# Where x is loaded and its statistics are made, in a fused forward and backward pass of an adaLN block with a 2-D Fourier filter

## The chip, the cores and the metric

The kernel runs on one core of a Trainium2 chip. The metric is the device time of one execution in microseconds (us); a run of the kernel is compared by its median. An engine is named as the profile names it: PE is TensorE's matmuls, PEld its weight loads, DVE is VectorE, ACT is ScalarE, POOL is GpSimd, SP is SyncE, which here only issues DMAs. Each engine takes its instructions from a queue of its own, in order.

## The reference

One block of a network, on 2048 tokens of 1024 channels, and its gradients for one grad_out. The inputs are bfloat16.

```
sa, ca, ga, sb, cb, gb = six rows of silu(c) @ w_mod
h = layernorm(x) * (1 + ca) + sa
x = x + ga * irfft2(rfft2(h) * (w_r + 1j * w_i))
h = layernorm(x) * (1 + cb) + sb
y = x + gb * (gelu(h @ w1 + b1) @ w2 + b2)
out = y and the gradients of y with respect to x, w_r, w_i, w1, b1, w2, b2, c, w_mod
```

w1 is 1024 by 3584. The two-dimensional Fourier transforms are made as matmuls with matrices of sines and cosines.

## The kernel before, in words

Tokens are worked in four tiles of 512 (128 partitions, 4 groups, 1024 channels). The program is written as one long list; a scheduler puts it into one fixed queue per engine, by the order in which the program has it, by priorities, and by what depends on what. `tc.issue_after(ins)` puts the instructions under it behind `ins`; `tc.high_priority()` draws them ahead.

**Loads at the start (SP's queue).** `mod_get`/`mod_load` (L269–271) bring half blocks of w_mod, 1 MB each, into the tiles wblk, of which there are three in a ring; `mod_block` (L273–284) multiplies such a half block by silu(c) on PE (the tile in PSUM is pm) and casts it into a row (L282). `load_tok` (L140–148) brings one of the four tiles of x, `x4s[0..3]` (x_0 to x_3 in the rows): half of it, 512 KB, by a plain DMA of SP (L144), and the rest in two gathers that POOL issues (L146). `load_go` (L351) brings one of four tiles of grad_out, 1 MB each: go0 and go1 have tiles of their own, the last two lie in `fbuf[:, 2]` and `fbuf[:, 3]`. `load_w2t` (L342) brings chunks of w2, transposed, into wt. Blocks 1 (1 + ca, `opca_row`) and 5 (gb, `gb_row`) of w_mod are needed first.

**The turns of grad_out.** gb's row is turned into a column (pc, L381; gb_col, L383). Then each tile of grad_out is transposed by 32 matmuls on PE (pt, L389), and every fourth finishes a bank of PSUM, which DVE (L393) and ACT (L397) by turns scale with gb_col and write to gBoT. The last turn's results let PE begin with pp: `ph_part` (L834–847) multiplies gBoT with w2's chunk `fc`, and ACT or DVE evicts the result (L845, into pho or phr). Seven chunks (fc 0 to 6) are ordered ahead of the spectral part; the rest, from L922 on, have no fixed place, and the scheduler lays them between later work. The other blocks of w_mod (pm) lie between them.

**The sines.** `trig` (L434–448, called ten times by `gen_mats`, L454–471) makes a matrix in three steps: POOL writes rows of indices (L419) into one of two buffers gidx, DVE takes them modulo a power of two by an AND (L446), ACT takes the sine (L447). Two small sines more make al (L467). A sine and a square root need different tables on ACT, which an ACT_TABLE_LOAD brings.

**Statistics and folds.** The loop at L862 goes over the four tiles of x. `ln_dve` makes mean and variance with BN_STATS on DVE (L493), `ln_mix` makes half of them so (L503) and half with two passes of ACT (L507, L510), `ln_act` all with ACT; each ends in `ln_fin`, with one Sqrt on ACT (L483) and two small operations on DVE. `norm_act` (L518) normalises on ACT into fbuf. The first tile takes `ln_dve`, the others `ln_mix`. Then DVE multiplies by `opca_row` and folds (all TENSOR_TENSORs of L195): `fold_tok` and `fold_d` or `fold_pair`, with x's tile as scratch, and at the end of each pair the row saf is added. A fold here is the sums and differences of mirrored tokens and channels that quarter the Fourier matmuls.

**The spectral part.** `spectral_core` begins with `s_fwd` (L531): pu (L542 for the matrices CE and SE, kept in smA) multiplies folded tiles by sines; CE's first pu are ordered behind the last pp of chunk 6 (`early_pe`, L541). After it come pcs (L581), the filter, pv and po (L774), and `consume_fwd` (L885), which adds to x, normalises twice on DVE and ACT, and writes n3 for the MLP. While it runs, PE has pp to do.

Of the kernel before, what the change touches and what calls it, by code (L numbers as in the profile page):

```python
# [35 lines left out]
def kernel(  # L36
# [39 lines left out]
    def ps_d(name):  # L76
        return psum.tile([P, 512], FP32, tag="d", name=name)
# [116 lines left out]
    def tt(out, a, b, op):  # L194
        return nc.vector.tensor_tensor(out=out, in0=a, in1=b, op=op)  # L195
# [154 lines left out]
    def load_go(j):  # L350
        nc.sync.dma_start(out=gos[j], in_=go_f[j * BW:(j + 1) * BW, :].rearrange("(a p) d -> p a d", p=P))  # L351
# [3 lines left out]
    def mod_get(r, h):  # L355
        wm[r, h] = mod_tile()
        mod_load(r, h, wm[r, h][:], nc.sync)

    mod_get(1, 0)
    load_tok(x4s[0], A_x, 0)  # L360
    mod_get(1, 1)
    mod_get(5, 0)
    for h in range(2):
        mod_block(1, h, wm[1, h][:])
# [13 lines left out]
    load_w2t(3)  # L378
    pc = ps_d("pc")
    for cch in range(NDC):  # L380
        nc.tensor.matmul(pc[:, cch:cch + 1], lhsT=gb_row[0:1, cch * P:(cch + 1) * P], rhs=ones_bf[0:1, 0:1], start=True, stop=True)  # L381
# [56 lines left out]
    def trig(dst, colv, rowv, nrow, width, modn, cosine):  # L438
        idx = gidx[:, gcount[0] % 2, :]
        gcount[0] += 1  # L440
        sh = float(3 * modn // 4 if cosine else modn // 2)
        for r in range(nrow):
            ov = idx[:, r * width:(r + 1) * width]
            pts(ov.rearrange("p (s w) -> p s w", s=2) if len(colv.shape) == 3 else ov, colv, rowv[r], sh, ALU.mult, ALU.add)
        n = nrow * width
        nc.vector.tensor_scalar(out=idx[:, 0:n], in0=idx[:, 0:n], scalar1=modn - 1, scalar2=None, op0=ALU.bitwise_and)  # L446
        nc.scalar.activation(out=dst, in_=idx[:, 0:n].rearrange("p (r w) -> p r w", w=width), func=ACT.Sin,  # L447
                             bias=negpi[:], scale=2 * np.pi / modn)
# [5 lines left out]
    def gen_mats():  # L454
        for cl, colv, modn in ((CE, kev, 2048), (SE, kev, 2048), (CO, kod, 4096), (SO, kod, 4096)):
            sm = (smA, smB)[cl % 2]
            rows, n = (rowo, 4) if cl % 2 else (rowe, 2)
            if cl == SE:
                nc.gpsimd.memset(kev[:, 0:1], 512.0)
            for r in range(0, n, 2):  # L460
                trig(sm[:, cl // 2, r:r + 2, :], colv, rows[r:r + 2], 2, 512, modn, cl < 2)
            if n == 2:
                nc.gpsimd.dma_start(out=d_SF[:, cl, 0:n], in_=sm[:, cl // 2])
        for cl, colv, modn in ((CE, jf[:, 0:256], 1024), (SE, jf[:, 1:257], 1024), (CO, jod, 2048), (SO, jod, 2048)):
            trig(em1[:, 0, 2 * cl:2 * cl + 2, :], colv, rowe, 2, 256, modn, cl < 2)
# [7 lines left out]
    def ln_act(x4, row, i, jk):  # L473
        sv = small.tile([P, 4, 4], FP32, tag="lnsv")
        for q in range(4):
            nc.scalar.activation(out=jk[:, q, :], in_=x4[:, q, :], func=ACT.Identity, accum_out=sv[:, q, 0:1])
        nc.vector.tensor_scalar(out=sv[:, :, 1:2], in0=sv[:, :, 0:1], scalar1=-1.0 / D, scalar2=None, op0=ALU.mult)
        for q in range(4):
            nc.scalar.activation(out=jk[:, q, :], in_=x4[:, q, :], func=ACT.Square, bias=sv[:, q, 1:2], accum_out=sv[:, q, 2:3])
        ln_fin(sv[:, :, 2:3], sv[:, :, 1:2], sv[:, :, 3:4], 1.0 / D, row, i)  # L480

    def ln_fin(var, nmean, std, scale, row, i):
        sqrt_in[0] = nc.scalar.activation(out=std, in_=var, func=ACT.Sqrt, bias=eps_c[:], scale=scale)  # L483
        rs = stats[:, row, 0, 4 * i:4 * i + 4].rearrange("p (q o) -> p q o", o=1)
        nc.vector.reciprocal(out=rs, in_=std)
        tt(stats[:, row, 1, 4 * i:4 * i + 4].rearrange("p (q o) -> p q o", o=1), nmean, rs, ALU.mult)

    def ln_dve(x4, row, i):
        st = small.tile([P, 4, 2, nc.vector.BN_STATS_DIM], FP32, tag="lnst", bufs=1)
        mv = small.tile([P, 4, 4], FP32, tag="lnmv")  # L490
        for q in range(4):
            for h in range(2):
                nc.vector.bn_stats(out=st[:, q, h, :], in_=x4[:, q, h * KH:(h + 1) * KH])  # L493
            nc.vector.bn_aggr(out=mv[:, q, 0:2], in_=st[:, q])
        nc.vector.tensor_scalar(out=mv[:, :, 2:3], in0=mv[:, :, 0:1], scalar1=-1.0, scalar2=None, op0=ALU.mult)
        ln_fin(mv[:, :, 1:2], mv[:, :, 2:3], mv[:, :, 3:4], 1.0, row, i)

    def ln_mix(x4, row, i, jk):
        st = small.tile([P, 4, 2, nc.vector.BN_STATS_DIM], FP32, tag="lnst", bufs=1)
        mv = small.tile([P, 4, 4], FP32, tag="lnmv")  # L500
        for q in range(2):
            for h in range(2):
                nc.vector.bn_stats(out=st[:, q, h, :], in_=x4[:, q, h * KH:(h + 1) * KH])  # L503
            nc.vector.bn_aggr(out=mv[:, q, 0:2], in_=st[:, q])
        nc.vector.tensor_scalar(out=mv[:, 0:2, 2:3], in0=mv[:, 0:2, 0:1], scalar1=-1.0, scalar2=None, op0=ALU.mult)
        for q in range(2, 4):
            nc.scalar.activation(out=jk[:, q, :], in_=x4[:, q, :], func=ACT.Identity, accum_out=mv[:, q, 0:1])  # L507
        nc.vector.tensor_scalar(out=mv[:, 2:4, 2:3], in0=mv[:, 2:4, 0:1], scalar1=-1.0 / D, scalar2=None, op0=ALU.mult)
        for q in range(2, 4):
            nc.scalar.activation(out=jk[:, q, :], in_=x4[:, q, :], func=ACT.Square, bias=mv[:, q, 2:3], accum_out=mv[:, q, 0:1])  # L510
        nc.vector.tensor_scalar(out=mv[:, 2:4, 1:2], in0=mv[:, 2:4, 0:1], scalar1=1.0 / D, scalar2=None, op0=ALU.mult)
        ln_fin(mv[:, :, 1:2], mv[:, :, 2:3], mv[:, :, 3:4], 1.0, row, i)

    def norm_act(out4, in4, row, i):
        norm_in[0] = ()
        for q in range(4):
            t = 4 * i + q
            norm_in[0] += (nc.scalar.activation(out=out4[:, q, :], in_=in4[:, q, :], func=ACT.Identity,  # L518
                                                scale=stats[:, row, 0, t:t + 1], bias=stats[:, row, 1, t:t + 1]),)

    sqrt_in, norm_in = [None], [()]
# [1175 lines left out]
```

## Time and profile before

| | us |
|---|---|
| time, median of 3 runs | 1399.26 (1396.29 to 1399.28) |
| the profiled execution: its time | 1398.61 |
| the profiled execution: its span | 1396.8 |
| PE busy in the span | 1351.6 |
| DVE busy | 1063.7 |
| ACT busy | 767.6 |
| POOL busy | 347.8 |
| TensorE clock granted, mean | 0.99 |

The span is what the profile sees, from its first instruction to its last; the rest of the execution's time lies around it. Busy times of different engines overlap. "PE pu L542 <- DVE fbuf L195" in a list of waits reads: PE's matmul of line 542, which writes pu, waited for DVE's instruction of line 195, which writes fbuf. In a timeline a row gives start, length, engine, line, operation, output<-input, shapes, how many in a run, and in brackets the idle time ahead and what ended it.

### The profile page before, as it was taken

Reading aid. Unit: us, or ns where it says so; the run is one execution under the profiler, and the core shown is the slowest. Engines: PE = TensorE matmul, PEld = TensorE weight load, DVE = VectorE, ACT = ScalarE, POOL = GpSimd, SP = SyncE. Lnnn points to the kernel's source line nnn. Section 1 sums busy time; section 2 is a strip of 40 time slices with the busy share of each in tenths; the row PEclk is TensorE's granted clock in tenths of the full one; section 3 lists DMA queues with packets and bytes.
Section 4 is the critical chain, followed back from the end, with each engine's and each line's share of the span. In section 5 each row is a group of like instructions: output and inputs, shape, how many; then the busy total and the mean of one; then the engine's idle time right before and its main releaser. Section 6 shows DMA issues by size and latency. Waiting matters only on the chain.

```text
span 1396.8 us, 18464 instructions
## 1 busy us (share of the span) xinstructions
PE 1351.6 (97%) x6774; PEld 657.6 (47%) x6899; DVE 1063.7 (76%) x1471; ACT 767.6 (55%) x1090; POOL 347.8 (25%) x434
## 2 busy tenths in 40 slices
PE   4998999999999999999999999999999999999998
PEld 2545566444444444444444444444654555444444
DVE  4997889977888787787811388889888489976990
ACT  4875657657977766656503684445732454534311
POOL 5410533301212122122111011011444320332351
PEclk8999999999999999999999999999999999999999
DMA  9982755899787777697999979988679978899991
GB/s 318 289 237 57 202 143 189 259 273 357 241 246 247 229 248 239 202 275 247 244 319 219 220 185 272 306 275 231 216 221 259 222 205 200 218 232 239 292 344 64
DMA packets 360689, 331.12 MB, mean 237 GB/s; under 512 B 207962, under 2 KB 303088, under 8 KB 360470
## 3 DMA queue, kind: packets, MB, share of 16 engines
q1 hardware_dynamic: 319702, 204.96, 56.9%
q0 software_dynamic: 35136, 119.73, 25.0%
q10 hardware_dynamic: 5760, 5.25, 1.2%
q8 instruction: 54, 0.88, 0.3%
q14 instruction: 37, 0.30, 0.1%
HBM read 165.73 MB, written 114.87 MB: 201 GB/s over the span
## 4 chain that ended last, share of the span: by engine, by line
PE 72%; DVE 7%; DMA 3%; issue 1%; ACT 1%; ACTq 0%; DVEq 0%
PE pg L1130 14%; PE gw1acc L1565 13%; PE gw2acc L1302 13%; PE pz L976 13%; PE pbo L1030 13%; DVE ct L195 4%; PE pp L839 2%; PE po L774 1%; DVE st L493 1%; PE pcs L581 1%; DMA hhsA<-d_hh 1%; DMA w2sA<-in_B_w_dram 1%; DMA d_n<-ct 1%; PE acc3a L218 1%; PE pu L542 1%
## 5 line engine op out<-in xcount | busy, mean ns | idle before, releaser
L839 PE MATMUL pp<-gBoT,wt 128*128 128x512 bf16 x874 | 197.9, 383 | 4.1 <-ACT phr L845 2.9
L1130 PE MATMUL pg<-w1T,gzr 128*128 128x512 bf16 x877 | 194.3, 379 | 1.3 <-issue 0.5
L1565 PE MATMUL gw1acc<-gzh,n3n 128*128 128x512 bf16 x626 | 139.1, 379 | 3.6 <-DVE ct L779 2.8
L839 PEld LDWEIGHTS <-wt 128*128 128x128 bf16 x896 | 88.0, 98 | 108.2 <-issue 7.3
L1565 PEld LDWEIGHTS <-n3n 128*128 128x128 bf16 x896 | 87.4, 98 | 108.2 <-issue 4.4
L1130 PEld LDWEIGHTS <-gzr 128*128 128x128 bf16 x896 | 86.6, 98 | 108.4 <-issue 5.8
L976 PEld LDWEIGHTS <-w 128*128 128x128 bf16 x896 | 87.3, 98 | 106.8 <-issue 2.4
L976 PE MATMUL pz<-n3Tb,w 128*128 128x512 bf16 x437 | 98.4, 379 | 1.6 <-DVE w2sD L1052 0.9
L976 PE MATMUL pz<-n3Ta,w 128*128 128x512 bf16 x439 | 98.0, 379 | 0.4
L195 DVE TENSOR_TENSOR ct<-ct 128x2048 bf16<-128x2048 bf16 (+1 forms) x84 | 91.6, 1119 | 7.1 <-DMA d_n<-ct 4.7
L1030 PEld LDWEIGHTS <-hhA 128*128 128x128 bf16 x608 | 58.9, 98 | 72.7 <-issue 2.5
L1302 PE MATMUL gw2acc<-gB,hhsA 128*128 128x512 bf16 x405 | 91.7, 379 | 0.6
L1569 ACT CAST gwo<-gw1acc 128x512 bf16<-128x512 f32 x56 | 32.2, 581 | 108.3 <-PE gw1acc L1565 87.8
L979 ACT ACTIVATE gt<-pz,b_col 128x512 bf16<-128x512 f32 x112 | 72.9, 682 | 33.3 <-PE pz L976 33.0
L987 ACT ACTIVATE gt<-gt 128x2048 bf16<-128x2048 bf16 x28 | 53.5, 1911 | 64.3 <-DVE gt L195 64.3
L195 DVE TENSOR_TENSOR gt<-gt,gt 128x2048 bf16<-128x2048 bf16 x56 | 68.6, 1224 | 19.8 <-ACT gt L989 18.5
L1310 ACT CAST gwo<-gw2acc 128x512 bf16<-128x512 f32 x40 | 23.6, 590 | 85.8 <-PE gw2acc L1302 85.8
L1302 PEld LDWEIGHTS <-hhsA 128*128 128x128 bf16 x416 | 40.7, 98 | 47.2
L1565 PE MATMUL gw1acc<-gzu,n3n 128*128 128x512 bf16 x251 | 55.2, 379 | 0.3
L983 ACT ACTIVATE gt<-gt 128x2048 bf16<-128x2048 bf16 x28 | 53.5, 1909 | 2.3 <-DVE hhC L195 1.6
L989 ACT ACTIVATE gt<-gt 128x2048 bf16<-128x2048 bf16 x28 | 53.4, 1907 | 0.4
L1302 PE MATMUL gw2acc<-gB,otl 128*128 128x512 bf16 x218 | 49.2, 379 | 0.4 <-issue 0.2
(371 smaller groups left out, 2511.0 us busy)
## 6 DMA issues: line engine op xcount, KB each, us to landing
gzr<-d_gz SPq DMA_DIRECT2D x28, 512.0 KB
wblk<-in_w_mod_dram SPq DMA_DIRECT2D x12, 1024.0 KB
d_ph<-pho POOLq DMA_DIRECT2D x21, 512.0 KB, 5.6
out_dram<-otl POOLq DMA_DIRECT2D x40, 256.0 KB, 4.8
d_hh<-hhA POOLq DMA_DIRECT2D x19, 512.0 KB, 5.0
wrw<-in_w_mod_dram SPq DMA_DIRECT2D x32, 256.0 KB
w<-in_B_w_dram SPq DMA_DIRECT2D x7, 1024.0 KB
hhC<-d_ph SPq DMA_DIRECT2D x14, 512.0 KB
```

The lines of the kernel that those rows point to most:

```text
L195: return nc.vector.tensor_tensor(out=out, in0=a, in1=b, op=op)
L839: last_pe[0] = nc.tensor.matmul(pp[:], lhsT=wt[:, fc % 4, cch, :], rhs=gBoT[j][:, cch, :], start=(cch == 0), stop=(cch == NDC - 1))
L976: last_pe[0] = nc.tensor.matmul(pz[:], lhsT=w1s[g][:, cch, k * P:(k + 1) * P], rhs=n3T[:, cch, :], start=(cch == 0), stop=(cch == NDC - 1))
L979: z_in = nc.scalar.activation(out=zb[:, k, :], in_=pz[:], func=ACT.Identity, bias=b1_col[:, fc:fc + 1], scale=1.0)
L983: nc.scalar.activation(out=av, in_=zb, func=ACT.Square)
L987: nc.scalar.activation(out=sg, in_=bv, func=ACT.Sigmoid, scale=2.0 * GK)
L989: nc.scalar.activation(out=bv, in_=bv, func=ACT.Sigmoid, scale=-2.0 * GK)
L1030: last_pe[0] = nc.tensor.matmul(pbs[i][:], lhsT=hh[:, k, i * P:(i + 1) * P], rhs=wp[:, k, :], start=False, stop=(g == 6 and k == 3))
L1130: last_pg[0] = nc.tensor.matmul(pgs[i][:], lhsT=gzs[b, g][:, k, i * P:(i + 1) * P], rhs=w1Ts[g][:, k, h * KH:(h + 1) * KH], start=(g == 0 ...
L1302: nc.tensor.matmul(acc[:], lhsT=hh_of(fc)[:, t, :], rhs=gBs[t // 4][:, t % 4, h * KH:(h + 1) * KH], start=(t == 0), stop=(t == NT - 1))
L1565: nc.tensor.matmul(acc[:], lhsT=n3ns[t // 4][:, t % 4, cch * P:(cch + 1) * P], rhs=gz2[t // 8][:, t % 8, :], start=(t == 0), stop=(t == NT ...
L1569: w1g["ev"] = nc.scalar.copy(out=ob, in_=acc[:])
```

## The change

The plain halves of all four tiles of x go ahead of gb's half blocks and grad_out in SP's queue. The functions for the statistics move up in the program, and all four tiles' statistics stand ahead of the turns: the second tile's on ACT alone (`ln_act`), the others' on DVE alone (`ln_dve`); `ln_mix` is left for later parts. The first two tiles are normalised there too, the last two in the loop of the folds. Every sine of `trig` and of al is ordered behind `x_sqrt`, the last square root of these statistics.

```
@@ loads
+    load_tok(x4s[0], A_x, 0)
     mod_get(1, 0)
-    load_tok(x4s[0], A_x, 0)
+    load_tok(x4s[1], A_x, 1)
     mod_get(1, 1)
+    load_tok(x4s[2], A_x, 2)
+    load_tok(x4s[3], A_x, 3)
     mod_get(5, 0)
     for h in range(2):
         mod_block(1, h, wm[1, h][:])
...
     load_go(0)
     load_w2t(0)
     load_w2t(1)
-    load_go(1)
-    load_tok(x4s[1], A_x, 1)
-    load_go(2)
-    load_go(3)
+    for j in range(1, 4):
+        load_go(j)
     for h in range(2):
         mod_block(5, h, wm[5, h][:])
-    load_tok(x4s[2], A_x, 2)
-    load_tok(x4s[3], A_x, 3)
     load_w2t(2)
     load_w2t(3)
...
+    for i in range(4):
+        if i == 1:
+            ln_act(x4s[i], 0, i, fbuf[:, i])
+        else:
+            with tc.issue_after(u_in.ins):
+                ln_dve(x4s[i], 0, i)
+    x_sqrt = sqrt_in[0]
+    for i in range(2):
+        norm_act(fbuf[:, i], x4s[i], 0, i)
     pc = ps_d("pc")
@@ trig
-        nc.scalar.activation(out=dst, in_=idx[:, 0:n].rearrange("p (r w) -> p r w", w=width), func=ACT.Sin,
-                             bias=negpi[:], scale=2 * np.pi / modn)
+        with tc.issue_after(x_sqrt.ins):
+            nc.scalar.activation(out=dst, in_=idx[:, 0:n].rearrange("p (r w) -> p r w", w=width), func=ACT.Sin,
+                                 bias=negpi[:], scale=2 * np.pi / modn)
@@ gen_mats
         for k in range(2):
-            nc.scalar.activation(out=al[:, k, :], in_=rown, func=ACT.Sin, scale=np.pi / (2048 << k))
+            with tc.issue_after(x_sqrt.ins):
+                nc.scalar.activation(out=al[:, k, :], in_=rown, func=ACT.Sin, scale=np.pi / (2048 << k))
@@ loop of the folds
-        if i == 0:
-            with tc.issue_after(u_in.ins):
-                ln_dve(x4, 0, i)
-        elif i > 0:
-            ln_mix(x4, 0, i, fb)
-        else:
-            ln_act(x4, 0, i, fb)
-        norm_act(fb, x4, 0, i)
+        if i > 1:
+            norm_act(fb, x4, 0, i)
         tt(fb, fb, bcn(opca_row, 4), ALU.mult)
         fold_tok(fb, x4)
```

What this does to the queues is seen at three places. First SP, from its first load of w_mod on, before; x_0 to x_3 are the tiles of x, go_142 and go_143 the first two of grad_out, fbuf its last two:

```order
L271 DMA wblk<-in_w_mod_dram 128x8x512
L144 DMA x_0_137<-in_A_x_dram 128x2x1024
L271 DMA wblk<-in_w_mod_dram 128x8x512 x2
L351 DMA go_142<-in_grad_out_dram 128x4x1024
L271 DMA wblk<-in_w_mod_dram 128x8x512
L342 DMA_TRANSPOSE wt<-in_B_w_dram 128x8x128 x2
L351 DMA go_143<-in_grad_out_dram 128x4x1024
L144 DMA x_1_138<-in_A_x_dram 128x2x1024
L351 DMA fbuf<-in_grad_out_dram 128x4x1024 x2
L144 DMA x_2_139<-in_A_x_dram 128x2x1024
L144 DMA x_3_140<-in_A_x_dram 128x2x1024
L342 DMA_TRANSPOSE wt<-in_B_w_dram 128x8x128 x2
```

And the same place of the changed kernel:

```order
L144 DMA x_0_137<-in_A_x_dram 128x2x1024
L271 DMA wblk<-in_w_mod_dram 128x8x512
L144 DMA x_1_138<-in_A_x_dram 128x2x1024
L271 DMA wblk<-in_w_mod_dram 128x8x512
L144 DMA x_2_139<-in_A_x_dram 128x2x1024
L144 DMA x_3_140<-in_A_x_dram 128x2x1024
L271 DMA wblk<-in_w_mod_dram 128x8x512 x2
L351 DMA go_142<-in_grad_out_dram 128x4x1024
L342 DMA_TRANSPOSE wt<-in_B_w_dram 128x8x128 x2
L351 DMA go_143<-in_grad_out_dram 128x4x1024
L351 DMA fbuf<-in_grad_out_dram 128x4x1024 x2
L342 DMA_TRANSPOSE wt<-in_B_w_dram 128x8x128 x2
```

Four plain halves of x stand ahead of all of grad_out now, where one did; go_142 went behind the last half block of gb.

Second DVE, among the folds of the first pair of tiles, before. The TENSOR_TENSORs are folds, the CASTs are evictions of pp, the rest are statistics of the third tile, x_2:

```order
L195 TENSOR_TENSOR fbuf<-x_0_137 128x2048
L508 TENSOR_SCALAR mv<-mv 128x2
L503 BN_STATS st<-x_2_139 128x6
L845 CAST pho<-pp 128x4x128
L195 TENSOR_TENSOR x_0_137<-fbuf 128x4x512 x2
L511 TENSOR_SCALAR mv<-mv 128x2
L504 BN_AGGR mv<-st 128x2
L195 TENSOR_TENSOR fbuf<-x_0_137 128x8x256
L845 CAST pho<-pp 128x4x128
L195 TENSOR_TENSOR fbuf<-x_0_137 128x8x256
L485 RECIPROCAL stats<-mv 128x4
L503 BN_STATS st<-x_2_139 128x6
```

In the changed kernel, where every line of the functions below `pc` is about ten higher (the AND is L504, the eviction of pp L855):

```order
L195 TENSOR_TENSOR fbuf<-x_0_137 128x2048
L195 TENSOR_TENSOR fbuf<-fbuf,rows_86 128x4096
L504 TENSOR_SCALAR gidx<-gidx 128x1024
L855 CAST pho<-pp 128x4x128
L504 TENSOR_SCALAR gidx<-gidx 128x1024
L195 TENSOR_TENSOR x_0_137<-fbuf 128x4x512
L855 CAST pho<-pp 128x4x128
L504 TENSOR_SCALAR gidx<-gidx 128x512 x2
L855 CAST pho<-pp 128x4x128
L195 TENSOR_TENSOR x_0_137<-fbuf 128x4x512
L504 TENSOR_SCALAR gidx<-gidx 128x512 x2
L195 TENSOR_TENSOR fbuf<-x_0_137 128x8x256 x2
```

The statistics are gone from between the folds, and ANDs of the sines stand there. Between the last turn of grad_out and the last fold stand 2 BN_STATS where 9 stood, 8 ANDs (4 of 1024 and 4 of 512 elements) where 6 stood (2 and 4), and 6 evictions of pp where 10 stood.

Third PE, at the begin of the spectral part, before; pp of the last chunk ahead of it, then the first pu:

```order
L839 LDWEIGHTS wt
L839 MATMUL pp<-gBoT_135,wt 128x512
L542 LDWEIGHTS fbuf
L542 MATMUL pu<-smA,fbuf 128x256
L542 LDWEIGHTS fbuf
L542 MATMUL pu<-smA,fbuf 128x256
L839 LDWEIGHTS wt
L839 MATMUL pp<-gBoT_132,wt 128x512
```

Behind these two pu stand 39 pp, and then the other six pu of this tile of PSUM. In the changed kernel (pp is L849, pu L552):

```order
L849 LDWEIGHTS wt
L849 MATMUL pp<-gBoT_135,wt 128x512
L552 LDWEIGHTS fbuf
L552 MATMUL pu<-smA,fbuf 128x256
L552 LDWEIGHTS fbuf
L552 MATMUL pu<-smA,fbuf 128x256
L552 LDWEIGHTS fbuf
L552 MATMUL pu<-smA,fbuf 128x256
L552 LDWEIGHTS fbuf
L552 MATMUL pu<-smA,fbuf 128x256
```

All eight pu stand together, and the next pp behind them. The number of pp is the same in all; 51 more of them stand in the long block beside `consume_fwd` (512 where 461 stood).

More of the change, by code (lines that the diff above doesn't have):

```diff
@@ L368, with ln_act @@
     load_w2t(1)
-    load_go(1)
-    load_tok(x4s[1], A_x, 1)
-    load_go(2)
-    load_go(3)
+    for j in range(1, 4):
+        load_go(j)
     for h in range(2):
         mod_block(5, h, wm[5, h][:])
-    load_tok(x4s[2], A_x, 2)
-    load_tok(x4s[3], A_x, 3)
     load_w2t(2)
     load_w2t(3)
+    def ln_act(x4, row, i, jk):
+        sv = small.tile([P, 4, 4], FP32, tag="lnsv")
+        for q in range(4):
+            nc.scalar.activation(out=jk[:, q, :], in_=x4[:, q, :], func=ACT.Identity, accum_out=sv[:, q, 0:1])
+        nc.vector.tensor_scalar(out=sv[:, :, 1:2], in0=sv[:, :, 0:1], scalar1=-1.0 / D, scalar2=None, op0=ALU.mult)
+        for q in range(4):
+            nc.scalar.activation(out=jk[:, q, :], in_=x4[:, q, :], func=ACT.Square, bias=sv[:, q, 1:2], accum_out=sv[:, q, 2:3])
+        ln_fin(sv[:, :, 2:3], sv[:, :, 1:2], sv[:, :, 3:4], 1.0 / D, row, i)
@@ new lines, in ln_fin, with ln_dve @@
+    def ln_fin(var, nmean, std, scale, row, i):
+        sqrt_in[0] = nc.scalar.activation(out=std, in_=var, func=ACT.Sqrt, bias=eps_c[:], scale=scale)
+        rs = stats[:, row, 0, 4 * i:4 * i + 4].rearrange("p (q o) -> p q o", o=1)
+        nc.vector.reciprocal(out=rs, in_=std)
+        tt(stats[:, row, 1, 4 * i:4 * i + 4].rearrange("p (q o) -> p q o", o=1), nmean, rs, ALU.mult)
+    def ln_dve(x4, row, i):
+        st = small.tile([P, 4, 2, nc.vector.BN_STATS_DIM], FP32, tag="lnst", bufs=1)
+        mv = small.tile([P, 4, 4], FP32, tag="lnmv")
+        for q in range(4):
+            for h in range(2):
+                nc.vector.bn_stats(out=st[:, q, h, :], in_=x4[:, q, h * KH:(h + 1) * KH])
+            nc.vector.bn_aggr(out=mv[:, q, 0:2], in_=st[:, q])
+        nc.vector.tensor_scalar(out=mv[:, :, 2:3], in0=mv[:, :, 0:1], scalar1=-1.0, scalar2=None, op0=ALU.mult)
+        ln_fin(mv[:, :, 1:2], mv[:, :, 2:3], mv[:, :, 3:4], 1.0, row, i)
@@ new lines, in ln_mix @@
+    def ln_mix(x4, row, i, jk):
+        st = small.tile([P, 4, 2, nc.vector.BN_STATS_DIM], FP32, tag="lnst", bufs=1)
+        mv = small.tile([P, 4, 4], FP32, tag="lnmv")
+        for q in range(2):
+            for h in range(2):
+                nc.vector.bn_stats(out=st[:, q, h, :], in_=x4[:, q, h * KH:(h + 1) * KH])
+            nc.vector.bn_aggr(out=mv[:, q, 0:2], in_=st[:, q])
+        nc.vector.tensor_scalar(out=mv[:, 0:2, 2:3], in0=mv[:, 0:2, 0:1], scalar1=-1.0, scalar2=None, op0=ALU.mult)
+        for q in range(2, 4):
+            nc.scalar.activation(out=jk[:, q, :], in_=x4[:, q, :], func=ACT.Identity, accum_out=mv[:, q, 0:1])
+        nc.vector.tensor_scalar(out=mv[:, 2:4, 2:3], in0=mv[:, 2:4, 0:1], scalar1=-1.0 / D, scalar2=None, op0=ALU.mult)
+        for q in range(2, 4):
+            nc.scalar.activation(out=jk[:, q, :], in_=x4[:, q, :], func=ACT.Square, bias=mv[:, q, 2:3], accum_out=mv[:, q, 0:1])
+        nc.vector.tensor_scalar(out=mv[:, 2:4, 1:2], in0=mv[:, 2:4, 0:1], scalar1=1.0 / D, scalar2=None, op0=ALU.mult)
+        ln_fin(mv[:, :, 1:2], mv[:, :, 2:3], mv[:, :, 3:4], 1.0, row, i)
@@ new lines, in norm_act @@
+    def norm_act(out4, in4, row, i):
+        norm_in[0] = ()
+        for q in range(4):
+            t = 4 * i + q
+            norm_in[0] += (nc.scalar.activation(out=out4[:, q, :], in_=in4[:, q, :], func=ACT.Identity,
+                                                scale=stats[:, row, 0, t:t + 1], bias=stats[:, row, 1, t:t + 1]),)
+    sqrt_in, norm_in = [None], [()]
+    for i in range(4):
[4 more added lines that the diff above has]
+                ln_dve(x4s[i], 0, i)
@@ L471, in gen_mats @@
         nc.gpsimd.dma_start(out=d_E[:], in_=em1[:])
[L473 to L521, printed above, removed]
     def behind(ins, later):
```

## The prediction

> **What bounds the kernel now.** I read the page's engine line and its slices first, then PE's waits, because PE is nearly always busy.
>
> ```profile
> PE 1351.6 (97%) x6774; PEld 657.6 (47%) x6899; DVE 1063.7 (76%) x1471; ACT 767.6 (55%) x1090; POOL 347.8 (25%) x434
> ...
> PE   4998999999999999999999999999999999999998
> ...
> PEclk8999999999999999999999999999999999999999
> ```
>
> PE is busy for 1351.6 of 1396.8 us, and its matmuls are the same in both kernels. So the change can move the time only through PE's 45 idle us and through the stretches in which PE is granted a lower clock. The waits from 0 to 330 us hold most of that idle time:
>
> ```profile
> PE pm L279 <- DMA wblk<-in_w_mod_dram: 12.0, 5, 4.6
> PE pu L542 <- DVE fbuf L195: 4.0, 1, 4.0
> PE pp L839 <- ACT phr L845: 2.9, 1, 2.9
> ...
> PE pt L389 <- DMA go<-in_grad_out_dram: 2.0, 1, 2.0
> ...
> PE pt L389 <- DMA fbuf<-in_grad_out_dram: 0.7, 1, 0.7
> ```
>
> The columns are total, times and longest. Three places can move: the loads ahead of the transposes (pt), the wait of the spectral part (pu) for the folds, and the late wait of pp for an eviction by ACT. The timeline of PE shows them in order of time:
>
> ```profile
> 33.17 3.75 PE L389 MATMUL pt<-ident,go 128*128 128x128 bf16 x32 [2.03 <-DMA go<-in_grad_out_dram]
> 37.66 6.18 PE L389 MATMUL pt<-ident,fbuf 128*128 128x128 bf16 x64 [0.74 <-DMA fbuf<-in_grad_out_dram]
> 43.83 5.34 PE L839 MATMUL pp<-gBoT,wt 128*128 128x512 bf16 x23
> 49.63 1.89 PE L279 MATMUL pm<-wblk,u_b 128*128 128x512 bf16 x8 [0.46 <-DMA wblk<-in_w_mod_dram]
> ...
> 101.09 7.07 PE L839 MATMUL pp<-gBoT,wt 128*128 128x512 bf16 x32
> ...
> 108.21 8.58 PE L839 MATMUL pp<-gBoT,wt 128*128 128x512 bf16 x38
> 120.77 1.46 PE L542 MATMUL pu<-smA,fbuf 128*128 128x256 bf16 x6 [3.97 <-DVE fbuf L195]
> ```
>
> Up to 43.83 PE follows grad_out's tiles as they land. From there it has pp enough until 116.8, and waits 3.97 us for the last fold. Three windows (length; then PE, PEld, DVE, ACT and POOL busy; clock; DMA share; GB/s) say who is full and where:
>
> ```profile
> 20.00:40.00 20.00, 13.57 (x108) 9.72 (x107) 13.98 (x38) 13.86 (x26) 5.36 (x8) 0.67 1.04 334
> 44.37:120.71 76.34, 70.69 (x323) 31.80 (x327) 72.76 (x108) 51.10 (x76) 20.78 (x26) 0.99 0.78 223
> 120.77:134.00 13.23, 13.20 (x87) 9.67 (x88) 5.94 (x7) 8.62 (x15) 0.00 (x0) 0.78 0.00 0
> ```
>
> From 20 to 40 us the DMA engines are full at 334 GB/s. From the last turn of grad_out (44.37) to the last fold (120.71) DVE is busy for 72.76 of 76.34 us, so DVE sets when the spectral part starts. Behind the wait PE runs 13.23 us at .78 of its clock.
>
> **Term 1, the loads.** Ahead of grad_out's last tile now stand the plain halves of x2 and x3, 0.52 MB each, which stood behind it. The halves that POOL gathers are issued from POOL's own queue in both kernels. So 1.05 MB more goes through full DMA engines at 334 GB/s: +3.1 us. SP's transposes of w2 move too, and go1 is queued behind them as before; gb's second half block has only 0.5 MB more ahead of it, which is the lower bound, 1.6 us. The upper one is 4.7, if x1's half, ahead of go2 already, counts again. I take 3.1, since the DMA share is 1.04: the last fbuf transposes come 3.1 us late, pp starts at 46.9 instead of 43.8, and DVE comes to its folds at 47.5 instead of 44.4. The statistics that now lie ahead of the turns go into DVE's and ACT's idle time (6 us each of the 20 in the window, and more before it), so I count them at nothing; without that cover eleven BN_STATS by 0.67 us, 7 us, would stand ahead of the turns.
>
> **Term 2, DVE from the turns to the last fold.** Groups of DVE from 44.37 to 120.77 (busy, mean ns | idle before):
>
> ```profile
> L503 DVE BATCH_NORM_STATS2 st<-x 128x6 f32<-128x512 bf16 x9 | 6.0, 679 | 0.0
> L845 DVE CAST pho<-pp 128x512 bf16<-128x512 f32 x8 | 5.5, 683 | 0.0
> ...
> L446 DVE TENSOR_SCALAR gidx<-gidx 128x512 int32<-128x512 int32 x4 | 1.7, 427 | 2.3 <-POOL gidx L419 2.3
> ...
> L446 DVE TENSOR_SCALAR gidx<-gidx 128x1024 int32<-128x1024 int32 x2 | 1.4, 691 | 0.0
> L504 DVE BATCH_NORM_AGGREGATE mv<-st 128x2 f32<-128x12 f32 x5 | 1.0, 201 | 0.0
> L508 DVE TENSOR_SCALAR mv<-mv 128x2 f32<-128x2 f32 x3 | 0.5, 150 | 0.0
> ```
>
> Nine BN_STATS become two: −7 × 0.67 = −4.7. Aggregates go from five to two (−0.6), and of three sets of small operations like L508's, five of 0.16 to a set, one of three is left (−2.0). DVE's evictions of pp ahead of the last fold go from ten to six: −4 × 0.68 = −2.7. One cast of a mod block goes to ACT (−0.7). Two more of the wide ANDs for the sines come behind the turns: +2 × 0.69 = +1.4; small work on al that waited for a sine comes behind too, some +0.8 by the 0.15 to 0.2 us of such operations. Sum −8.5: 64.3 us of work, which from 47.5 ends at 111.8 if nothing waits.
>
> **The added wait.** Ten sines, all ordered behind the last Sqrt of x, leave two index buffers full until then; eight ANDs then stand among the folds in DVE's queue, and behind each the rest of the folds. In the trace before, four do, and they wait 2.3 us in all:
>
> ```profile
> DVE gidx L446 <- POOL gidx L419: 2.3, 4, 0.9
> DVE fbuf L195 <- ACT fbuf L518: 1.1, 1, 1.1
> ```
>
> By that mean, 0.57 us, eight wait 4.6; the bounds are 0 (the rows are ready in time) and 10.8 (the narrow ones wait the longest, 0.9, and the wide ones, with twice the elements, 1.8). I take 4.6, the mean of what stands nearest. The 1.1 us for ACT's normalised tile I keep, since two of the tiles are still normalised beside the folds. The last fold ends at 111.8 + 4.6 + 1.1 = **117.5**, 3.2 us earlier than before.
>
> **What PE does with it.** PE is at its first pu by 108.0 + 3.1 = 111.1 at the latest, and waits until 117.7. Before, 39 pp (the 8.58-us row) stood between the first two pu and the other six and filled most of such a wait; now all eight pu stand together, and these pp come behind. They still have to be done. So against the 120.77 of before, PE stands at 117.5 + 0.2 + 8.6 − 120.77 = **+5.5 us**. PE is idle about 6.6 us instead of 4.0, plus the 3.1 of the loads: the same 5.5 to within rounding. A clock stretch like that at 120.77 follows in both.
>
> The Trainium skill has a rule that bears on this, in "TensorE: Matmul & The Clock Gate", section "HAM oscillation — how this bites in real kernels": no gap in PE's work over some 3.4 us, or the clock falls. The 3.97-us wait with .78 behind it agrees; by the rule a wait that fell below 3.4 us would give back what that stretch cost, and a longer one would change nothing. The next rows show .79 behind a wait of 2.87 us, so here the row speaks against taking 3.4 as the limit, and no term of mine uses it.
>
> **Term 3, the late wait.** At 316.73 PE waits 2.87 us for an eviction by ACT, whose queue stands behind a Sqrt that waits 8.33 us for DVE:
>
> ```profile
> 294.61 1.28 DVE L845 CAST pho<-pp 128x512 bf16<-128x512 f32 x2
> 300.62 2.36 DVE L195 TENSOR_TENSOR ct<-ct 128x2048 bf16<-128x2048 bf16 x2 [4.73 <-DMA d_n<-ct]
> ...
> 315.90 0.30 ACT L483 ACTIVATE mv<-mv,eps_c 128x4 f32<-128x4 f32 x1 [8.33 <-DVE mv L494]
> ...
> 316.73:324.88 8.15, 8.10 (x29) 3.33 (x30) 8.08 (x10) 6.30 (x8) 1.32 (x3) 0.79 1.06 379
> ```
>
> Between 295.9 and that Sqrt DVE evicts nothing. Now the spectral chain starts 3 us earlier, 51 more pp stand in the block that lies beside this chain, and the evictions are dealt out anew between ACT and DVE, so that the Sqrt should no longer hold PE. I take −2.9. The bounds are 0 (another eviction is caught behind another Sqrt) and −4.6 (the 8.15 us at .79 run at full clock too, 8.15 × .21 = 1.7).
>
> **Sum**, against the profiled execution's 1398.61 us (span 1396.8, 1.8 around it): +5.5 − 2.9 = +2.6, **1401.2 us**. That run lies 0.65 below the median, 1399.26, so it is +1.9 us, 0.14%, against the median. About 0.3%, 4.2 us, is what a measurement of this kernel can tell from no change: 1395.1 to 1403.5. The change is thus worth what the last fold's end is worth: time ≈ 1398.6 + (that end − 114.9).
>
> **Rivals.**
>
> *The index rows become the bound (slower).* POOL makes the rows between the sines, and its operations take longer beside DVE's folds:
>
> ```profile
> 14.46 1.82 POOL L419 TENSOR_SCALAR genv<-genv 128x256 f32<-128x256 f32 x6
> ...
> 45.88 3.02 POOL L419 TENSOR_SCALAR gidx<-genv 128x512 int32<-128x512 f32 x4 [5.54 <-ACT smB L447]
> 50.11 6.05 POOL L419 TENSOR_SCALAR gidx<-genv 128x256 int32<-128x256 f32 x6 [1.21 <-ACT smB L447]
> ```
>
> Six of 256 columns took 1.82 us while DVE made statistics, and 6.05 among the folds. If the wide ANDs suffer likewise, the eight wait 4 × 1.8 + 4 × 0.9 = 10.8 us, the last fold ends at 123.7, and the time is 1398.6 + 8.8 = 1407.4. It decides from 119.75 on, that is where the eight wait over 6.8 us together. For it: the rows above. Against it: while DVE waits, it is not in POOL's way. The Trainium skill states the mechanism in "SBUF — State Buffer", section "Who interferes with whom": a DVE instruction with two inputs in SBUF and a GpSimd instruction that reads SBUF take the same port, and whichever starts second is blocked for the whole of the other. It speaks against this change, and the 6.05-us row agrees; the four 512-column rows in 3.02 us, mostly ahead of the first fold at 49.27, agree too. By it alone the time would be this rival's.
>
> *The late wait stays.* Then the time is 1398.6 + 5.5 = 1404.1. For it: the same chain of Sqrts stands in ACT's queue. Against it: DVE has less to do ahead of it and PE more.
>
> *DVE is free in time (faster).* The eight ANDs and the folds wait for nothing, the last fold ends at 111.8, PE waits under 1 us there, and neither clock stretch follows: −3.1 by the formula, −13.23 × .22 = −2.9 and −1.7: 1390.9. Against it: four such ANDs wait already.
>
> *The change does not reach the time.* The loads fit between others and PE's wait stays what it was: 1398.6.
>
> **How the numbers follow.** My forecast has 0.40, the slow index rows 0.26, the late wait that stays 0.14, the free DVE 0.15, no effect 0.05. Forecast and no effect are within 0.3% (0.45), slow rows and late wait slower (0.40), the free DVE faster (0.15). The forecast's own range is 1397.9 to 1402.8 (Term 1 by 1.6 either way, the late clock stretch below). The range for 8 in 10 takes in both far rivals, the slow one with the upper bound of Term 1: 1391 to 1409.
>
> **What would show it.** The last turn's transposes some 3 us late; the last fold's end near 117.5; a pu wait near 6.6 us, put down to DVE fbuf; gidx waits on DVE near 4.6 us; no pp wait on ACT near 317. It is wrong if the statistics delay the turns, if the gidx waits lie far from 4.6, or if a wait appears beside the consume part that the trace before does not have.

## The result and the profile after

| | us |
|---|---|
| before, median of 20 runs | 1396.27 (1392.55 to 1402.53) |
| changed, median of 20 runs | 1401.49 (1398.13 to 1407.42) |
| ratio | 1.0036, 95% interval 1.0024 to 1.0048 |
| changed, the profiled execution: its time | 1398.77 |
| changed, the profiled execution: its span | 1397.0 |

The changed kernel is slower by 0.36%, that is 5 us by the medians. The forecast was a time of 1401.2, which the median meets, but by luck: it started from a kernel before that three runs had put at 1399.26. Against the 20-run median the cost is 5.2 us where +1.9 was forecast (2.6 against the profiled execution). So the sum has to be taken apart, and for that the profiles show more than their ends: the two profiled executions end only 0.2 us apart, 1396.8 and 1397.0.

First the engines and slices of the changed kernel's page:

```profile
PE 1357.7 (97%) x6899; PEld 655.3 (47%) x6899; DVE 1062.9 (76%) x1466; ACT 767.6 (55%) x1087; POOL 355.1 (25%) x434
...
PE   4998999999999999999999999999999999999998
...
PEclk9999999999999999999999999999999999999999
```

At this grain there is no difference to see: the shares are those of before. PE's waits over the whole execution (total, times, longest) show it:

```profile
PE pm L279 <- DMA wblk<-in_w_mod_dram: 12.0, 4, 5.6
PE pu L552 <- DVE fbuf L195: 6.1, 1, 6.1
PE pm L279 <- issue: 3.0, 1, 3.0
PE pt L447 <- DMA go<-in_grad_out_dram: 2.2, 1, 2.2
...
PE pp L849 <- ACT pho L855: 1.8, 2, 0.9
PE pp L849 <- DMA wt<-in_B_w_dram: 1.8, 1, 1.8
PE pp L849 <- DVE pho L855: 1.3, 2, 0.8
```

The wait at pu grew from 4.0 to 6.1 us, the one late wait of 2.9 for ACT is gone, and four short waits of pp and one for a transposed chunk of w2 have come. In PE's timeline, in order of time:

```profile
34.57 3.26 PE L447 MATMUL pt<-ident,go 128*128 128x128 bf16 x32 [2.23 <-DMA go<-in_grad_out_dram]
...
44.20 2.11 PE L849 MATMUL pp<-gBoT,wt 128*128 128x512 bf16 x9
47.57 1.89 PE L279 MATMUL pm<-wblk,u_b 128*128 128x512 bf16 x8 [1.26 <-DMA wblk<-in_w_mod_dram]
...
71.29 1.89 PE L849 MATMUL pp<-gBoT,wt 128*128 128x512 bf16 x8 [0.85 <-DVE pho L855]
...
78.17 1.89 PE L849 MATMUL pp<-gBoT,wt 128*128 128x512 bf16 x8 [0.93 <-ACT pho L855]
...
111.39 0.27 PE L552 MATMUL pu<-smA,fbuf 128*128 128x256 bf16 x1
117.72 1.67 PE L552 MATMUL pu<-smA,fbuf 128*128 128x256 bf16 x7 [6.05 <-DVE fbuf L195]
...
313.23 12.25 PE L849 MATMUL pp<-gBoT,wt 128*128 128x512 bf16 x56 [0.88 <-ACT pho L855]
327.23 2.98 PE L849 MATMUL pp<-gBoT,wt 128*128 128x512 bf16 x13 [1.75 <-DMA wt<-in_B_w_dram]
```

A good mark for how far PE has come is the first matmul of the MLP, pz: up to it PE has the same 832 pp and 96 pm and the same Fourier matmuls to do in every kernel here. Before:

```profile
327.04 7.07 PE L976 MATMUL pz<-n3Ta,w 128*128 128x512 bf16 x32
```

Changed:

```profile
330.69 7.07 PE L980 MATMUL pz<-n3Ta,w 128*128 128x512 bf16 x32
```

So the changed kernel is 3.65 us behind at pz. That lag is still 3.6 us in the middle of the MLP (a wait for w2sD ends at 448.59 and at 452.22, one for w2sA at 707.73 and at 711.35) and 3.2 us at 1265 us. It is lost from sight at one place, a wait near 1278 us, behind which the two are 0.2 us apart. This row is of the kernel before; the changed kernel's profiled execution has no such wait:

```profile
1277.93 17.43 PE L1565 MATMUL gw1acc<-gzh,n3n 128*128 128x512 bf16 x79 [2.83 <-DVE ct L779]
```

### The profile page after: what moved, and what is told of

It reads as the page before. It is cut to its first block, busy times and chain, and to the rows that moved or that the text cites. A ratio compares the mean times of both kernels' runs of the same rounds, so it can differ in the third digit from the quotient of the medians.

```text
span 1397.0 us, 18588 instructions
## 1 busy us (share of the span) xinstructions
PE 1357.7 (97%) x6899; PEld 655.3 (47%) x6899; DVE 1062.9 (76%) x1466; ACT 767.6 (55%) x1087; POOL 355.1 (25%) x434
## 4 chain that ended last, share of the span: by engine, by line
PE 70%; DVE 9%; ACT 2%; DMA 2%; issue 1%; POOL 0%; DVEq 0%; ACTq 0%
PE pg L1134 14%; PE gw2acc L1306 14%; PE gw1acc L1569 14%; PE pbo L1034 11%; PE pz L980 11%; DVE ct L195 4%; DVE gt L195 2%; PE pp L849 2%; PE po L784 1%; PE pcs L591 1%; PE pu L1449 1%; ACT gt L991 1%; DMA w2sA<-in_B_w_dram 1%; DMA wt<-in_B_w_dram 1%; DVE st L398 1%
## 5 line engine op out<-in xcount | busy, mean ns | idle before, releaser
L849 PE MATMUL pp<-gBoT,wt 128*128 128x512 bf16 x896 | 198.2, 379 | 5.0 <-ACT pho L855 1.8
L849 PEld LDWEIGHTS <-wt 128*128 128x128 bf16 x896 | 87.4, 98 | 108.8 <-issue 4.6
L855 ACT CAST pho<-pp 128x512 bf16<-128x512 f32 x60 | 34.3, 582 | 38.2 <-PE pp L849 37.0
```

The lines of the kernel that those rows point to most:

```text
L849: last_pe[0] = nc.tensor.matmul(pp[:], lhsT=wt[:, fc % 4, cch, :], rhs=gBoT[j][:, cch, :], start=(cch == 0), stop=(cch == NDC - 1))
L855: nc.any.tensor_copy(out=ov, in_=pv)
```

## Experiments

All runs below were timed in five rounds beside the kernel before (its medians there: 1397.24, 1397.94, 1396.9), but for one more execution of the kernel before. Since the times spread over 10 us, the reading goes by the first pz as well as by the medians.

**The order of the sines taken back.** In `trig` and for al:

```
-        with tc.issue_after(x_sqrt.ins):
-            nc.scalar.activation(out=dst, ... func=ACT.Sin, ...)
+        nc.scalar.activation(out=dst, ... func=ACT.Sin, ...)
```

> The changed kernel without the order of the sines behind the last square root of x. PE's queue stays what it was, and eight ANDs still stand on DVE behind the turns. Theory A (the folds' end and the 39 pp that came behind the eight pu set the time, the order of the sines little): the ANDs wait about as long as in the changed kernel (5.7 us), the last fold ends within 1.5 us of 117.7, time within 2 us of the changed kernel. Rival B (the order of the sines is what costs, through the ANDs' waits among the folds): the waits fall to some 2.3 us as before, the last fold ends near 114.3, and the time is 3 to 4 us below the changed kernel's.

Measured: 1401.11 (ratio to before 1.0016, 0.9997 to 1.0035), within 0.4 us of the changed kernel by the medians; by the ratios it is 2.8 us nearer to the kernel before, and the two intervals overlap, so a small price of the order is not excluded. The eight ANDs wait 5.8 us, the wait at pu is 5.4 and ends at 116.31, the first pz is at 328.80, 1.9 us earlier. Theory A holds: without the order the ANDs still stand behind the turns, and wait. So what leaves them there is the rest of the change, the early place of the statistics and loads. The loads alone do not: in the next run four ANDs wait, 2.5 us in all, about as before.

**Only the loads.** The kernel before with SP's new order, statistics and sines where they were:

```
+    load_tok(x4s[0], A_x, 0)
     mod_get(1, 0)
...
-    load_tok(x4s[2], A_x, 2)
-    load_tok(x4s[3], A_x, 3)
```

> The kernel before with only the order of the loads changed; statistics and sines stay in the loop of the folds. The scheduler leaves 17 pp between the first two pu and the other six (39 before, none in the changed kernel). Theory A (pp left behind pu): by 22 pp of 0.22 us, 4.8 us come behind the wait, the last fold may end up to 2 us earlier; time +2 to +4 us against before. Rival C (the loads themselves cost, by grad_out's tiles coming 3 us late): the last turn ends near 47 instead of 44 and the time is +3 us even where the last fold does not move. Rival D (the loads cost nothing): within 1 us of before.

Measured: 1416.21 (1.0119, 1.0092 to 1.0147), 19 us slower than before, and no theory had that. Its PE waits:

```profile
PE pp L838 <- ACT phr L844: 7.1, 1, 7.1
PE gw1acc L1564 <- DVE ct L778: 4.8, 1, 4.8
PE pu L541 <- DVE fbuf L195: 4.6, 1, 4.6
PE pt L388 <- DMA go<-in_grad_out_dram: 3.6, 1, 3.6
PE pz L975 <- DVE w2sD L1051: 3.2, 1, 3.2
```

The grad_out wait of 3.6 us and the pu wait are the front's part; the rest is late. At the front rival C's turns and theory A's folds are both there: PE begins pp at 47.03, 3.2 us later than before, and the pu wait ends at 119.52, 1.25 us earlier, with 22 more pp behind it. The first pz is at 334.40, 7.4 us later. DVE waits 10.2 us for the store of n3 (d_n), in whose buffer it works next, ACT's queue stands behind a Sqrt that needs DVE, and PE waits 7.1 us for ACT. Only the loads were changed, yet what the scheduler made of the rest differs too (17 pp at pu where 39 stood), so this run prices the loads together with that. Of the 12 us that it loses behind pz, the waits for w2sD and ct are a part; the rest stays open.

**One chunk more of pp ahead of pu.**

```
-    PH_EARLY = 6
+    PH_EARLY = 7
```

In the changed kernel:

> The changed kernel with seven chunks of pp ordered ahead of the last early one instead of six, so that 32 more pp (7.1 us) stand ahead of the first pu. Theory A: PE comes to pu at about 118.5, after the last fold, the wait of 6.1 us for DVE is gone, and the time falls by 5 to 6 us against the changed kernel, to or below that of before. Rival E (the loss lies later, in waits beside the consume part, and an earlier spectral part is worth something): the wait at pu goes but comes back later as waits of pp or of the consume chain; time within 2 us of the changed kernel.

Measured: 1405.25 (1.0054, 1.0029 to 1.0079), no faster than the changed kernel: by the ratios 2.5 us slower, with overlapping intervals. The pu wait is gone, and another has come:

```profile
120.43 1.03 PE L552 MATMUL pu<-smA,fbuf 128*128 128x256 bf16 x8 [1.32 <-DVE U L813]
300.91 26.94 PE L849 MATMUL pp<-gBoT,wt 128*128 128x512 bf16 x110 [4.96 <-DVE pho L855]
...
454.38 3.57 PE L980 MATMUL pz<-n3Tb,w 128*128 128x512 bf16 x8 [3.50 <-DVE w2sD L1056]
```

Here DVE waits 6.6 us for the store d_n, 1.8 in the changed kernel, and PE waits 5 us for DVE. The first pz comes 3.0 us earlier (327.69), and 2.6 of that go at w2sD, where 6.8 us of slow clock come too. Theory A predicted the front, that the pu wait goes; its 5 to 6 us did not come. Rival E, that the wait comes back later, is nearer; the 2 us that it allowed lie inside what these runs can tell apart. Filler pulled ahead of pu does what was expected there, and the part beside the consume chain and behind it takes more than that back.

In the kernel before, as a control:

> Control: the kernel before with seven chunks ahead instead of six. 64 + 7 pp stand ahead of the six pu that wait, where 32 + 39 stood, the same number. Theory A: PE comes to them at the same time and waits the same 4 us; time within 1 us of before. Rival F (a chunk more ahead of pu is worth its 7 us anywhere, for instance by another order of evictions): 4 us or more faster than before.

Measured: 1396.52 (0.9992, 0.9973 to 1.0011), no difference, as theory A had it; the pu wait is 3.95.

**The store of n3 by POOL.**

```
-        nc.sync.dma_start(out=chunk_rows(d_n3, i), in_=tmp)
+        nc.gpsimd.dma_start(out=chunk_rows(d_n3, i), in_=tmp)
```

With seven chunks, in the kernel before, and in the changed kernel:

> The changed kernel with seven early chunks, and the store of n3 (d_n) issued by POOL instead of SP, so that it is not queued among SP's transposes of w2 and loads of w1. Theory G (the gain of the filled pu wait was lost because DVE waits for this store, 6.6 us, and PE then 5.0 for DVE's eviction, with a slow clock behind): the d_n wait of DVE falls under 2 us, PE's pp wait near 300 is gone with its slow clock, and the time falls by 6 us or more against the kernel with seven chunks and SP's store (1405), to 1399 or less. Rival H (the store is slow whoever issues it, since the DMA engines are full): the d_n wait stays over 4 us and the time within 3 us of 1405.

> The kernel before with the store of n3 issued by POOL. Theory G: the late pp wait of 2.9 us behind the d_n wait of 4.7 goes, 2 to 4 us faster than before. Rival H: within 1 us of before.

> The changed kernel with the store of n3 issued by POOL: the late race is then alike in this and in the kernel before with POOL's store. Theory A (the change's loss lies at the spectral part's begin: 2 us more of waiting at pu, 2 us of short waits for evictions behind the ANDs, and a slow clock behind every pu wait of 6 us): this kernel stays 3 to 6 us slower than the kernel before with POOL's store. Rival I (the change's loss is the late part's): the two are within 1.5 us.

Measured: 1403.22 (1.0026, 1.0005 to 1.0047), 1401.18 (1.0016, 0.9993 to 1.0039) and 1404.40 (1.0044, 1.0021 to 1.0067). DVE's d_n wait is 6.2, 7.4 and 3.3 us; the pp wait behind it 4.58, 5.85 and 1.65. Theory G falls, and rival H holds for the wait: the store is as late from another queue. The changed kernel is 3.2 us above the kernel before with the same edit, as theory A said, though the intervals of the two overlap and in the profiled executions their first pz are level (330.45 and 330.31): in that execution of the kernel before, the late wait of 5.85 us lies ahead of pz, with 6.8 us of slow clock.

**The kernel before, profiled again.**

> The kernel before, unchanged, profiled once more, to see which of its waits and slow-clock stretches come back in another execution. Theory J (the slow clock behind a wait of about 4 us comes in some executions and not in others): the waits at pu and at pp are there within 1 us of 4.0 and 2.9, but at least one of the two slow stretches at 121 and 317 us is gone or of another length. Rival K: the waits themselves are what varies, by over 1.5 us.

Measured, one run: 1404.68. At pu PE waits 3.99 us, at pp 4.15, at gw1acc 6.61 (2.83 in the first profile), and behind each the clock is slow. So the pu wait is steady and the two late ones vary by 1.3 and 3.8 us. That is rival K for gw1acc; for pp it lies between J's 1 us and K's 1.5. Theory J's missing slow clock is not seen in this execution. The gw1acc wait is behind a load xt<-d_gx: SP issues it at 1272.40 in this execution, at 1268.41 in the first profile and at 1267.43 in the changed kernel's.

**That load by POOL, to take it out of SP's queue.**

```
-        x1_in = nc.sync.dma_start(out=n1, in_=chunk_rows(d_gx1, i))
+        x1_in = nc.gpsimd.dma_start(out=n1, in_=chunk_rows(d_gx1, i))
```

> The kernel before, with one load near its end (xt<-d_gx, whose late landing makes PE wait between 0 and 6.6 us for DVE near 1280 us, with a slow clock behind the longer waits) issued by POOL instead of SP, so that it is not queued among SP's transposes. Theory L (this wait is the lottery that spreads the times of all these kernels over 10 us): the gw1acc wait falls under 1 us, the median lies 3 to 6 us under that of before, and the runs spread less. Rival M (it waits as long whoever issues it): the median within 1.5 us of before, the wait still there.

> The changed kernel with the same load issued by POOL. With the lottery near 1280 us out of both kernels, what is left is the part up to the MLP. Theory A (the change's cost lies there): 3 to 5 us slower than the kernel before with the same load by POOL. Rival N (the change's cost is in how the late wait falls): within 1.5 us of it.

Measured: 1402.19 for the kernel before with it (1.0041, 1.0022 to 1.0060), 1408.70 for the changed one (1.0087, 1.0063 to 1.0110). As a cure it failed, both are slower: the gw1acc wait is gone, and PE waits for DVE between 1210 and 1243 us instead, 5.5 and 6.0 us in all. So neither theory L nor rival M had it. But the two differ by 6.5 us, and their marks by 6.8, 323.54 and 330.31: this is theory A's direction, and more than its 3 to 5 us. Rival N falls.

**Seven chunks, that load by POOL, and w1 later.**

```
-            load_w1({24: 1, 25: 1, 27: 5}.get(fc, 0))
+            load_w1({27: 7}.get(fc, 0))
```

> The changed kernel with seven early chunks, the late load by POOL, and all seven loads of w1 issued after chunk 27 instead of two of them beside the store of n3. Theory O (the loads of w1 on the full DMA engines are what makes the store of n3 late, and so PE's 5-us wait near 300 in the kernels with seven early chunks): DVE's d_n wait falls under 3 us, the pp wait near 300 under 1.5, no slow clock there, and the time falls to 1390 to 1394, under that of both kernels. Rival H (other transfers take their place): d_n wait over 4 us, time no better than the changed kernel with the late load by POOL.

Measured: 1407.30 (1.0077, 1.0059 to 1.0094). The d_n wait is 6.8 us, the pp wait near 300 5.18. Theory O falls: the loads of w1 are not what makes the store late.

**POOL's rows taken away.**

```
-        for r in range(nrow):
+        for r in range(nrow if gcount[0] <= 2 else 0):
```

> The changed kernel with the late load by POOL; it leaves out POOL's index rows of all sines but the first two, whose rows stand in the buffers for the rest, so the matrices are not the reference's. Beside the folds POOL then makes no rows, and an AND waits only until ACT's sine has read its buffer. Theory A (the waits behind POOL's rows put the folds off one for one, and the spectral part with them): the gidx waits fall from 5.7 to 1 to 3 us, the last fold ends 3 to 5 us earlier, the waits of PE for evictions near 71 and 78 us go, the pu wait falls to 2 to 3 us, and the first pz comes 3 to 5 us earlier. Rival P (the folds' end is not what counts): the first pz within 1 us of the changed kernel's.

This kernel leaves out the index rows of eight of the ten sines that `trig` makes, so its matrices are not the reference's, and only its times say something.

Measured: 1395.90 (0.9993, 0.9975 to 1.0012), 12.8 us under the same kernel with the rows (1408.70). PE's waits from 44 to 330 us, with the rows:

```profile
PE pu L552 <- DVE fbuf L195: 6.0, 1, 6.0
PE pp L849 <- DMA wt<-in_B_w_dram: 1.8, 1, 1.8
PE pp L849 <- ACT pho L855: 1.8, 2, 0.9
PE pp L849 <- DVE pho L855: 1.7, 2, 1.2
```

And without:

```profile
PE pu L552 <- DVE fbuf L195: 1.9, 1, 1.9
PE pp L849 <- DVE pho L855: 0.9, 1, 0.9
```

These four waits have shrunk or gone. On DVE the ANDs wait 6.1 us with the rows, and not at all without. The pu wait ends at 110.95 instead of 117.13, 6.2 us earlier: one for one with the ANDs' 6.1, while DVE's work up to there is nearly the same (66.00 and 65.14 us from 45 us on). So the waits put the folds off, and not slower folds. The first pz comes at 318.98 instead of 330.31, 11.3 us earlier, more than theory A's 3 to 5. To the folds' 6.2 us come the late waits of 0.88 and 1.82 us, of which 0.92 is left, the slow clock behind the pu wait, 2.7 us, and 0.7 for three pp that the scheduler put between the first two pu and the rest: 11.4 in all. It also put the ANDs nearer together in this kernel, so this is not the rows alone.

## Why the prediction came out as it did

**The folds came out right by luck, two errors against each other.** The last fold was forecast to end at 117.5, and PE started behind it at 117.72; its wait was 6.05 for 6.6. But DVE began its folds at 45.9, not 47.5, and was held longer:

```profile
45.91:117.66 71.75, 62.01 (x284) 27.40 (x282) 64.63 (x84) 39.31 (x53) 33.43 (x33) 0.99 0.72 217
```

64.63 us of work, where 64.3 were counted (ten small operations of 0.16 us, which the sum has as 2.0, are 1.6), in 71.75 us: 7.1 idle, where 5.7 were. The ANDs waited 5.7 us (4.6 forecast):

```profile
DVE gidx L504 <- POOL gidx L477: 5.7, 8, 1.4
```

Rows of POOL, one and four operations of 512 columns, say why:

```profile
54.12 2.87 POOL L477 TENSOR_SCALAR gidx<-genv 128x512 int32<-128x512 f32 x1
...
61.96 6.81 POOL L477 TENSOR_SCALAR gidx<-genv 128x512 int32<-128x512 f32 x4
```

Four took 6.81 us beside the folds, where one took 0.69 in the kernel before, ahead of them (16.70 us). The longest of the four, 3.66 us, ends 0.5 us behind a DVE product of two inputs (fbuf<-fbuf,rows) that lasts from 63.95 to 66.23; one at 57.73, while DVE waits at an AND, took 0.68. This is the mechanism of the first rival, and of the rule in the Trainium skill, "SBUF — State Buffer", section "Who interferes with whom"; the trace agrees that it acts here, not that it is the whole: the rival's 10.8 us of waits were twice what came. The rival's argument against itself, that POOL is not held up while DVE waits, is what the row of 0.68 us shows. The run without the rows shows that it is these waits that put the folds off.

Two rows that the prediction showed for this rival mix shapes, since a timeline gives a run of operations the shape of its first. The six in 1.82 us are two of 256 columns (0.42 us each) and four of 128, and the four in 3.02 us are two of 512 and two of 256. The six in 6.05 us are all of 256, and the shortest of these took 0.48: beside the folds the rows took twice as long, and not the three times that 1.82 against 6.05 suggests.

**Term 1, the loads, was too large where it was measured.** PE began pp at 44.20, 0.4 us later than before, not 3.1: go1's transposes began 1.4 us later, but the later tiles of grad_out came while DVE and ACT still worked, and the waits for fbuf went. The lower bound, 1.6, was too high as well. With the loads alone, in the second experiment, pp did begin 3.2 us later, at 47.03; there go1's transposes begin at 36.55 instead of 34.57, with the same order of SP's loads, and why is not shown. The cover for the statistics held, though with little left: in 20 to 40 us DVE is now busy for 17.86 and ACT for 17.95 us.

```profile
20.00:40.00 20.00, 13.47 (x112) 8.76 (x112) 17.86 (x50) 17.95 (x33) 0.00 (x0) 0.91 1.10 333
```

**What the forecast left out: evictions behind the ANDs.** DVE evicts pp too. While it waits at an AND, PE runs out of free banks: 0.85 and 0.93 us at 71 and 78, and 0.45 more between them. The prediction named only the folds as what is queued behind an AND. That PE came to its first pu at 111.39, where 111.1 was forecast, is luck again: these 2.2 us stand against the 2.7 by which Term 1 was too large.

**Term 3 failed in its size.** The Sqrt no longer holds PE for 2.87 us, as forecast, but 0.88 us for ACT and 1.75 for a chunk of w2 came in its place: −0.2 us instead of −2.9. With the measured size the forecast's own sum is +5.5 − 0.2 = +5.3 us, beside 5.2 by the medians. So two errors against each other are enough to meet the time: Term 3 was 2.7 us too low, and the 1398.61 that it was added to lies 2.3 us above the kernel's 20-run median.

Over all executions that wait is a matter of the store d_n: DVE waits 1.8 to 10.2 us for it in all but the one without rows, which has no such wait, and in the eight executions where it waits over 3.5 us, PE's wait behind it is 1.5 to 3.1 us shorter than DVE's. What makes the store late is not settled: it is neither SP's queue nor the loads of w1.

**"A clock stretch like that at 120.77 follows in both" holds for the two profiled executions, but not from one execution to the next.** In the trace's record of the clock the slow stretches come as half speed for 3.4 or 6.8 us (10.2 at times in the first 50 us). A stretch begins up to 3.3 us ahead of a wait's end, or up to 1.4 us behind it. With the 6-us pu wait of the changed kernel and its variants (6.05, 6.07, 6.00, and 5.44 with the sines free) 6.8 us came each time. With the 4-us wait of the kernel before and its variants it was 6.8 in three executions (3.97, 3.98, 3.99), 3.4 in one (3.98) and none in one (3.95). From that last, the kernel before with seven chunks:

```profile
120.27:134.00 13.73, 13.45 (x106) 10.35 (x108) 7.81 (x10) 10.48 (x18) 0.00 (x0) 1.00 0.07 15
```

Against the changed kernel's:

```profile
117.72:131.00 13.28, 13.24 (x90) 9.82 (x91) 6.54 (x10) 8.15 (x14) 0.00 (x0) 0.81 0.01 2
```

.81 of the clock over 13.28 us is 2.5 us. The profiled execution of before was one in which both its waits were followed by a slow clock: 2.9 us (13.23 × .22) and 1.7 (8.15 × .21). This accounts for the profiled pair: +5.3 + 2.5 − 4.6 = 3.2 of the 3.65 us at pz. Against the kernel before with seven chunks, which had no slow clock, it is 5.3 + 2.5 = 7.8 of 8.3. The variants of the kernel before with no slow clock and with one of 3.4 us had their first pz at 322.36 (seven chunks) and 323.54 (the late load by POOL), the kernel before itself in its two profiles at 327.04 and 327.66; the changed kernel had 330.69 and its variants with the rows and six chunks, sines behind the square root, 330.45 and 330.31. So the lag at pz is 3 us against the slower executions of before and 7 to 8 against the faster ones, and the 5.2 us of the medians lie between. How often each came in the twenty runs, and so what the clock adds to Term 3's error in the medians, is not shown. This chance and the gw1acc wait, 0 to 6.6 us in the kernel before and its variants and 0 to 5.2 in the changed one and its variants, may also be what lies between before's two medians, 1399.26 of 3 runs and 1396.27 of 20; that was not tested by itself.

**The rivals.** The slow index rows were the right mechanism at half the price. The late wait, which had 0.14, stayed in effect: 2.6 of its 2.9 us are there, but not for the reason named. Its +5.5 on the 20-run median would be 1401.8, as near to the measured time as the forecast, so the time does not decide between the two and the waits speak for the rival. DVE's queue was free of waits at the ANDs only with the rows taken away. That the change would do nothing is excluded by the interval.

The rule on gaps in the Trainium skill ("TensorE: Matmul & The Clock Gate", "HAM oscillation — how this bites in real kernels", some 3.4 us) is borne out in its direction and not as a limit: from 50 us on, no slow clock came with waits of PE up to 1.96 us in any execution here, with those of 2.1 to 4.0 us it did in most and not in all (2.10, 2.32 and 2.87 with, 2.83, 2.98 and 3.15 without), and with those of 4.1 us and more always.

## What to carry to other kernels

Work that is moved ahead frees an engine only as far as nothing else sinks into its place: here seven BN_STATS left the folds, two more ANDs came, and eight ANDs waited where four had. And what an earlier end is worth depends on the filler: the folds ended 3 us earlier, and 8.6 us of pp that had filled the wait for them came behind it. Before a gain on the filled engine is counted, list everything in its queue behind each wait, evictions too, and look where the scheduler's filler went, since filler pulled ahead at one place is missing at another. And where a wait is near the length at which the clock falls, one profile is one draw: several executions of the kernel before belong to the forecast. A time that meets the forecast can still hide two errors, so check the terms.

## What was not expected of the hardware

The slow clock comes in whole steps of 3.4 us at half speed, one to three in a row, so that the same 4-us wait cost nothing in one execution and 6.8 us at half speed in another. A POOL operation of 512 columns took 0.69 us at the start of the kernel before and up to 3.66 beside DVE's folds in the changed one. And a store of 1 MB held DVE up for 1.8 us in the changed kernel, 4.7 and 6.0 in two executions of the kernel before, and 10.2 with only the loads at the start in another order.
